# First feed-forward layer of groups 8 to 11: two groups at a time, seven block products of 256 columns in place of eight

## The chip, the core and the metric

The kernel runs on one core of a Trainium2 chip. Its engines work side by side, each through its own queue in order: TensorE (PE, matrix products into PSUM; its weight loads, PEld, overlap them), VectorE (DVE), ScalarE (ACT), GpSimd (POOL) and SyncE (SP), which issues DMAs. The metric is the device time of one execution in microseconds. One more execution was recorded by the hardware profiler.

## What is computed

The reference is block-sparse attention followed by a feed-forward block. B = 4 batches, 8 heads, S = 768 positions, head size 64; model width 512, hidden width 2048.

```python
scores_l = scale * q @ k.T      # kept where |pos_i - pos_j| < 16, else -1e9
scores_s = scale * q @ block_max(k).T + log(32)
a = softmax(concat([scores_l, scores_s]))
x = a @ concat([v, block_mean(v)])
xn = (x - mean) / sqrt(var + 1e-6) * g_ln
out = x + relu(xn @ w_ch1) @ w_ch2
```

## The kernel before

**Tiles.** The 3072 rows are 24 tiles T of 128 rows. Attention works on half tiles t = 0 to 47, four heads each, tile T = t // 2. The feed-forward part works on groups g = 0 to 11 of two tiles.

**Attention.** The first batch (t below 12) works in fp32. From t = 12 on, `load_q` and `load_k` load and split operands into an fp16 high and low part, `qk` makes the scores in PSUM, `softmax` takes the minimum on DVE, a step on POOL and the exponential on ACT into the tile `p`. `transp` casts `p` to fp16 with its residue and transposes both by a DMA on SP. `load_v` splits the values, and `pv` multiplies, adds the parts with a DVE reduction into the tile `x` of the row tile and scales it on POOL. There are XB = 6 buffers for x, so tile T + 6 takes the buffer of tile T, once that is stored.

**Normalisation.** `norm(T)` is `ln`, which writes the normalised tile `xn` (two buffers), and `lnT`, which from tile 4 on casts it to fp16 on ACT, takes the residue on DVE and transposes both with one DMA into `xs`, one tile per group and two buffers.

**Feed-forward.** All weights are held in SBUF as fp16 high and low parts, `wt[1, n]` for the first layer (n = 4 k + c: block k of 512 hidden units, chunk c of 128 of the 512 model columns) and `wt[2, f]` for the second. `g1(s)` with s = 8 g + j makes 256 hidden units for the 256 rows of a group. For each 128 hidden units, 12 matmuls of 256 columns run: four chunks, each high x high, low x high, high x low. ACT then writes `hh` (relu, fp16) and DVE `hl` (the residue). HB = 9 buffers of each let the first layer run ahead. `g2(s)` adds that block to two PSUM accumulators of 512 columns, one a row tile, 12 matmuls in all. After four and after eight blocks DVE adds an accumulator to `x` (it is "drained"), and after eight SP stores x to `out_x`.

**Order.** Every operation is recorded by a planner and nothing is issued when it is called. The planner (`Plan`) knows which operations need which, through tiles and the reuse of their buffers; it simulates the five engines with costs of its own, ranks operations by how late they could start, and repeats this 32 times (`ROUNDS`). What it has then is a fixed order for each engine. So all matmuls have the same line in the profile, L375, the helper that issues them. Extra waiting time that the planner allows for comes from `slack`. The place where a step is called sets which buffer it gets and what it depends on, but not when it runs. In the program's text, group g was called at t = 4 g + 4, when its two tiles are complete.

**Buffers by turn.** `HOMES` lists for some kinds of tile the memory that is taken in turn: three places for `ksg` (loaded k), four for `kh`, two each for `qs`, `p16`, `pT` and `bst`. PSUM has four pools ("s", "o", "h", "a") of two banks. Scores use s, value products o, the first layer h, the second a; the last group's second tile has a further accumulator in o, so that the end can go out in halves.

Of the kernel before, what the change touches and what calls it, by code (L numbers as in the profile page):

```python
# [23 lines left out]
P = 128  # L24
# [21 lines left out]
WARMV = 4  # L46
WARM = 36
PVS = 4


SEQ = [(1 + m // 8 % 2, m % 8 + m // 16 * 8) for m in range(2 * NF)]
# [21 lines left out]
WORDER = (  # L73
# [25 lines left out]
class Plan:  # L99
# [159 lines left out]
    def slack(self, x, y):  # L259

        name, a = self.names[x.stage]
        if x.engine == "tensor":
            if name in ("g1", "g2"):
                return SLACK2 * (a[0] >= 24)
            return SLACK * (name in ("qk", "pv", "batch_s"))
        late = name in ("load_q", "load_k", "load_v", "softmax", "transp", "pv") and a[0] >= LATE
        late |= name[:5] == "batch" and a[0] >= 2
        late |= name in ("ln", "lnT") and a[0] >= LATE // 2
        late |= name in ("g1", "g2") and a[0] >= 24
        if not late:  # L270
            return 0.0
        return SLACKD if y.dma else SLACKE
# [107 lines left out]
def body(ctx: ExitStack, tc, qt, qa, qe, kt, ks, va, vb, vs, g_ln, w1, w2, blocks, out):  # L380
    pl = Plan()
    cp = ctx.enter_context(tc.tile_pool(name="const", bufs=1))
    wp = ctx.enter_context(tc.tile_pool(name="work", bufs=1))
    pools = {n: ctx.enter_context(tc.tile_pool(name="ps" + n, bufs=2, space=bass.MemoryType.PSUM)) for n in "soha"}

    def work(tag, name, shape, dt=F32, bufs=1):
        return pl.tile(wp, shape, dt, tag, name, bufs)

    def psum(tag, name, shape):
        return pl.tile(pools[tag], shape, F32, tag, name, 2)  # L390


    wt = {}

    msk = cp.tile([P, 3, NC], F32, name="msk")
# [3 lines left out]
    tails = [cp.tile([P, 2, 2, NV2], F32, name=f"vst{i}") for i in range(NV)]  # L399
    vst = [x.rearrange("p h v x -> p (h v x)")[:, : 8 * D].rearrange("p (i j d) -> p i j d", i=2, j=4) for x in tails]  # L400
# [18 lines left out]
    kx = [work(f"kx{x}", f"kx{x}", [P, 2, NE])[:] for x in range(2)]  # L419

    emask = work("qke", "emask", [P, 3, NE])[:]

# [34 lines left out]
    @pl.step  # L457
    def go_late():
        late["p"] = prob[0], work("k0_0", "p3", [P, 4, NE])
        for x in late["p"]:  # L460
            nc.gpsimd.memset(x[:, :, NC:], 0.0)
        for i in range(2):
            late["v", i] = work(f"v16_{i}", f"v16_{i}", [P, 2, 4, 2, D], F16)

    def queue(*key):
        return nc.scalar if any(key[: len(x)] == x for x in BESIDE) else nc.sync

    turn = {}

    def home(kind):  # L470
        n = turn[kind] = turn.get(kind, -1) + 1
        return HOMES[kind][n % len(HOMES[kind])]

    stg_n = [0]

    def stg(tag, shape, dt=F32):
        stg_n[0] += 1
        if tag == "bst1":
            tag = ("bst", "qs")[stg_n[0] % 2]
        elif tag in ("bst", "qs"):  # L480
            tag = home(tag)
        return work(tag, f"{tag}{stg_n[0]}", shape, dt, 1 + (tag == "xn"))


# [127 lines left out]
    @pl.step  # L612
    def load_q(t):

        T, hh = divmod(t, 2)
        qs = stg('qs', [P, 4, P])
        for half in range(2):
            nc.sync.dma_start(qs[D * half : D * half + D], qt[T, hh])
        qhl = work(f"qhl{t % 2}", f"qhl{t}", [P, 4, P], F16)
        sc = bt["s", T // NT][:, 1:2]  # L620
        nc.scalar.activation(qhl[:], qs[:], AF.Copy, scale=sc)
        nc.vector.scalar_tensor_tensor(qhl[:D], qs[:D], sc[:D], qhl[:D], ALU.mult, ALU.subtract)
        st[t, "q"] = qhl

    @pl.step
    def load_k(t, pr):
        T, hh = divmod(t, 2)
        b = T // NT
        ksg = work(home("ksg"), f"ksg{t}_{pr}", [P, 2, NC])
# [4 lines left out]
        kh = work(home("kh"), f"kh{t}_{pr}", [P, 2, NC], F16)  # L634
# [33 lines left out]
    @pl.step  # L668
    def softmax(t, pr):
        T = t // 2  # L670
        var = 0 if T % NT == 0 else (2 if T % NT == NT - 1 else 1)
        if pr == 0:
            st[t, "p"] = (prob if t < NEARLY else late["p"])[t % 2]
            st[t, "mn"] = work("mn", f"mn{t}", [P, 4], F32, 2)
            if t >= NEARLY:
                st[t, "sum"] = work("sum", f"sum{t}", [P, 4], F32, 2)
        p, mn, sm, ps = st[t, "p"], st[t, "mn"], st.get((t, "sum")), st[t, "s", pr]
        if t < NEARLY:
            heads = [(2 * pr + v, emask[:, var] if v else msk[:, var]) for v in range(2)]
            for v, (j, mk) in enumerate(heads):  # L680
                w = mk.shape[1]
                nc.vector.tensor_tensor_reduce(
                    p[:, j, :w], ps[:, v, :w], mk, -QSCALE, 3.0e38, ALU.add, ALU.min, mn[:, j : j + 1]
                )
            for j, mk in heads:
                x = p[:, j, : mk.shape[1]]
                nc.scalar.activation(x, x, AF.Exp, bias=mn[:, j : j + 1], scale=-1.0)
            return
        mk = bt["mask", T // NT][:, var]
        for u in range(2):  # L690
            j = 2 * pr + u
            nc.vector.tensor_tensor_reduce(
                p[:, j, :NC], ps[:, u], mk, -1.0, 3.0e38, ALU.add, ALU.min, mn[:, j : j + 1]
            )
        m2, (scale, plus) = mn[:, 2 * pr : 2 * pr + 2], bt["c", T // NT]
        nc.gpsimd.tensor_scalar(m2, m2, plus, 0.0, ALU.mult, ALU.add)
        for u in range(2):
            j = 2 * pr + u
            x = p[:, j, :NC]
            nc.scalar.activation(x, x, AF.Exp, bias=mn[:, j : j + 1], scale=scale, accum_out=sm[:, j : j + 1])  # L700

    @pl.step
    def transp(t):

        p = st[t, "p"]
        p16 = work(home("p16"), f"p16_{t}", [P, 4, 3, P], F16)
# [5 lines left out]
        pT = work(home("pT"), f"pT_{t}", [P, 12, P], F16)  # L712
# [252 lines left out]
    def g2(s):  # L965
# [7 lines left out]
        for i in range(2):  # L973
# [3 lines left out]
            for c, ps in enumerate(acc[i]):  # L977
# [16 lines left out]
                if j == 7:  # L994
                    nc.sync.dma_start(out[T * P : T * P + P, cs], xt[T][:, cs])

    @pl.step
# [41 lines left out]

    def norm(T):  # L1040
        ln(T)
        lnT(T)

    def batch(b):
        for hp in range(4):
# [120 lines left out]
```

## Time and profile before

| | |
|---|---|
| time, median of 3 | 633.95 us (633.9 to 635.35) |
| the profiled execution | 633.53 us, of which the span is 631.7 |
| PE busy | 612.3 us, 97% of the span |
| DVE, ACT, POOL busy | 434.8, 388.2, 212.2 us |
| mean granted PE clock | 0.997 |

The span runs from the first to the last instruction of the recorded execution. A row of the profile names an engine, an operation, and "out<-in" by the program's tiles without their numbers: `h<-xs,wp` is a first-layer matmul, `a<-wp,hh` and `a<-wp,hl` a second-layer one, `o<-v,pT` a value product, `s<-kh,qhl` a score. PE's matmuls are pipelined, so one matmul's own duration is longer than the distance to the next; the distance is what counts for a sum.

### The profile page before, as it was taken

To read this page: it belongs to the slowest core of one execution; us is meant where nothing else is said; L and a number is where in the kernel's file an instruction comes from. 1 tells how busy PE (TensorE), PEld (TensorE's weight loads), DVE (VectorE), ACT (ScalarE), POOL (GpSimd) and SP (SyncE) were. 2 spreads that over 40 slices of the span, in tenths; PEclk is the share of its full clock that TensorE was granted. 3 is DMA by queue.
4 is the path that set the end of the run, shared out by engine and by line. 5 is a ranking of instruction groups with operands and counts; after the bars stand their busy time and mean duration, and the time that the engine had idled before them with its cause. 6 is when DMAs were issued, how large, how long until landed. Compare 5 with 4: busy or idle time off the path is not lost.

```text
span 631.7 us, 13448 instructions
## 1 busy us (share of the span) xinstructions
PE 612.3 (97%) x4678; PEld 435.7 (69%) x4678; DVE 434.8 (69%) x1160; ACT 388.2 (61%) x988; POOL 212.2 (34%) x417
## 2 busy tenths in 40 slices
PE   6899999999999999999999999999999999999997
PEld 5587777675776777666677677667766766666665
DVE  3799999898889999767976766756756744321212
ACT  3698899768998959778774664764663642110100
POOL 5131132022556537534643353533523512100000
PEclk8999999999999999999999999999999999999999
DMA  8990378535999887897755555756646423110000
GB/s 259 337 325 9 105 226 311 184 88 156 249 240 223 192 197 183 170 244 197 191 138 148 125 109 128 150 122 139 151 106 127 108 52 65 20 51 0 20 15 34
DMA packets 126628, 93.15 MB, mean 147 GB/s; under 512 B 84960, under 2 KB 109024, under 8 KB 126560
## 3 DMA queue, kind: packets, MB, share of 16 engines
q1 hardware_dynamic: 124928, 91.50, 56.3%
q10 hardware_dynamic: 1632, 0.79, 0.4%
q8 instruction: 37, 0.61, 0.4%
q14 instruction: 31, 0.25, 0.1%
HBM read 66.27 MB, written 6.29 MB: 115 GB/s over the span
## 4 chain that ended last, share of the span: by engine, by line
PE 56%; DVE 18%; DMA 13%; ACT 5%; issue 4%; POOL 3%; SPq 1%; ACTq 0%; DVEq 0%; POOLq 0%
PE a L375 26%; PE h L375 23%; PE o L375 3%; DMA ksg<-in_kt 3%; PE s L375 2%; DVE wp L375 2%; DVE wf L375 2%; DVE p L375 2%; DMA raw<-in_w 2%; ACT p L375 2%; DVE hl L375 2%; DMA vw<-in_va 2%; DVE x L375 2%; DMA bst<-in_ks 2%; DVE kl L375 2%
## 5 line engine op out<-in xcount | busy, mean ns | idle before, releaser
L375 PE MATMUL h<-xs,wp 128*128 128x256 f16 x2304 | 273.1, 273 | 1.8 <-DMA xs<-x 1.1
L375 PEld LDWEIGHTS <-wp 128*128 128x128 f16 x2304 | 223.8, 98 | 44.1 <-issue 1.8
L375 PE MATMUL a<-wp,hh 128*128 128x512 f16 (+1 forms) x768 | 226.5, 377 | 0.8 <-DVE x L375 0.8
L375 PE MATMUL a<-wp,hl 128*128 128x512 f16 x384 | 144.7, 377 | 0.0
L375 ACT ACTIVATE hh<-h 128x512 f16<-128x512 f32 x96 | 56.8, 592 | 128.6 <-PE h L375 106.6
L375 DVE SCALAR_TENSOR_TENSOR hl<-h,hh 128x512 f16<-128x512 f32 x96 | 65.8, 686 | 91.4 <-ACT hh L375 91.4
L375 PEld LDWEIGHTS <-hh 128*128 128x128 f16 x784 | 75.8, 98 | 64.5 <-issue 1.6
L375 ACT ACTIVATE p<-p,mn,sv 128x184 f32<-128x184 f32 x144 | 76.3, 533 | 20.4 <-POOL mn L375 17.1
L375 POOL TENSOR_TENSOR p<-p,p 128x512 f16<-128x512 f32 x72 | 71.8, 1006 | 25.8 <-ACT p L375 22.1
L375 PEld LDWEIGHTS <-hl 128*128 128x128 f16 x392 | 38.3, 98 | 44.6
L375 DVE CUSTOM_DVE_ANT_0 p<-s,mask 128x184 f32<-128x184 f32 x144 | 43.2, 343 | 21.5 <-PE s L375 21.4
L375 POOL TENSOR_SCALAR mn<-mn,sv 128x2 f32<-128x2 f32 x72 | 33.6, 469 | 66.7 <-DVE mn L375 66.6
L375 ACT ACTIVATE kh<-ksg,sv 128x368 f16<-128x368 f32 x72 | 42.9, 597 | 16.6 <-POOL ksg L375 16.5
L375 DVE SCALAR_TENSOR_TENSOR x<-a,wsc,x 128x512 f32<-128x512 f32 (+1 forms) x48 | 35.3, 738 | 23.6 <-PE a L375 23.6
L375 POOL TENSOR_TENSOR x<-x,rc 128x256 f32<-128x256 f32 x36 | 29.1, 809 | 65.3 <-DVE x L375 65.3
L375 DVE SCALAR_TENSOR_TENSOR kl<-ksg,sv,kh 128x368 f16<-128x368 f32 x72 | 46.3, 668 | 0.1
L375 POOL COPY ksg<-ksum 128x48 f32<-128x48 f32 x72 | 22.0, 307 | 68.1 <-DMA ksg<-in_kt 66.1
L375 ACT CAST p<-p 128x512 f16<-128x512 f32 x72 | 33.6, 509 | 0.4
L375 DVE TENSOR_REDUCE x<-o 128x256 f32<-128x512 f32 x36 | 24.4, 680 | 10.6 <-PE o L375 10.6
L375 DVE SCALAR_TENSOR_TENSOR v<-vst,sv,v 128x512 f16<-128x512 f32 x36 | 27.2, 761 | 0.7 <-ACT v L375 0.7
L375 PEld LDWEIGHTS <-pT 128*128 128x128 f16 x432 | 23.4, 98 | 6.2 <-DMA pT<-p 2.7
L375 PEld LDWEIGHTS <-qhl 128*128 128x128 f16 x288 | 24.0, 98 | 5.2
(127 smaller groups left out, 790.4 us busy)
## 6 DMA issues: line engine op xcount, KB each, us to landing
raw<-in_w SPq DMA_DIRECT2D x32, 512.0 KB, 7.9
ksg<-in_kt SPq DMA_DIRECT2D x72, 184.0 KB, 2.8
out_x<-x SPq DMA_DIRECT2D x23, 256.0 KB, 3.3
qw<-in_qt SPq DMA_DIRECT2D x36, 128.0 KB, 3.0
vst<-in_va SPq DMA_DIRECT2D x36, 128.0 KB, 2.4
qs<-in_qt SPq DMA_DIRECT2D x36, 128.0 KB, 2.8
vst<-in_vb SPq DMA_DIRECT2D x84, 32.0 KB, 2.0
bst<-in_ks SPq DMA_DIRECT2D x12, 192.0 KB, 2.6
```

Of the source, the lines that this page charges most:

```text
L375: getattr(getattr(nc, self.ops[i].engine), op)(*a, **k)
```

## The change

Groups 8 to 11 become two pairs, pn = 4 (tiles 16 to 19) and pn = 5 (tiles 20 to 23). The 512 rows of a pair are two block rows: the even tiles and the odd tiles, 256 rows each. The 512 model columns are two block columns, and 512 hidden units (block k) two blocks of 256. So the first layer of block k is a 2 x 2 block product, which takes eight block products of 12 matmuls each (256 hidden units, 256 rows, 256 model columns in high and low parts). `sp1` makes it from seven, by Winograd's form of Strassen's scheme:

- `combine(k, c)`, called eight times at t = 24, adds high and low parts of two weight chunks on POOL, makes four combinations on DVE and splits them again (ACT, DVE) into `tt[k, c]`, in memory that the first batch and the raw weights used.
- `split1(T)` (even tiles) and `split2(T)` (odd tiles) take the place of `lnT` from tile 16 on. They make a11, a12, a22 and four combinations s1 to s4 of the two tiles, each cast, with residue, and transposed by DMA; pair 4 has 5 transposes per two tiles, pair 5 has 7.
- `sp1(pn, k)` runs the seven products with three PSUM banks. The sums x and z go on growing after they have been read: `note` copies an intermediate sum on ACT, and three DVE additions join the sums. `keep` writes hh and hl.
- `sp2` is the second layer for one block row, with the same number of matmuls as `g2`. `pair_ffn` calls it so that the odd tiles follow every second block.
- Pairs are called at t = 8 pn + 8, that is 40 and 48.

To make room: HB is 8. `kh` has three homes, one of them in the memory of the first batch's kx, beside the scratch tile "room". From t = 42 (`ONE`) on, ksg, qs, p, p16 and pT have a single buffer each (`ALONE`), since pair 5's operands take the second ones. Tiles 22 and 23 have x in `msk` and in `qw4`, not among the six buffers. From t = 28 value products use one PSUM bank, o0. The planner gets slack for the new steps.

```diff
-HB = 9
+HB = 8
+SP = 4
+ONE = 42
-    kh=("kh0", "kh1", "kx0", "kx1"),
+    kh=("kh0", "kh1", None),
+ALONE = dict(ksg=("qke",), qs=("qs",), p16=("p2",), pT=("pta",))
+WD = (("vw0", "vw1"), ("vw2", "vw3"), ("vw4", "vw5"), ("qw2", "qw3"))
+OPS = {
+    4: dict(a11="xs", a12="xs", a22="qw5", s2="xs", s4="xs", s3="room", s1="tail"),
+    5: dict(a11="bst", a12="qw1", a22="k0_0", s2="k0_1", s4="k0_2", s3="k0_3", s1="qw0"),
+}
+XHOME = {22: "msk", 23: "qw4"}
+SLACKP = 500
...
+            if name in ("sp1", "sp2"):
+                return SLACK2 if name == "sp2" or self.names[y.stage][0] != "sp1" else SLACKP
...
-            st[t, "p"] = (prob if t < NEARLY else late["p"])[t % 2]
+            st[t, "p"] = (prob if t < NEARLY else late["p"])[t % 2 if t < ONE else 0]
...
-        ps = psum("o", f"o{t}", [P, 4, 2, D])
+        ps = psum("o", f"o{t}", [P, 4, 2, D], 0 if t >= 8 * SP - 4 else None)
...
-            xt[T] = work("x", f"x{T}", [P, DM], F32, XB)
+            xt[T] = work(XHOME[T], f"x{T}", [P, DM]) if T in XHOME else work("x", f"x{T}", [P, DM], F32, XB)
...
+    def combine(k, c):
+        top, low = (wt[1, 4 * k + 2 * i + c] for i in range(2))
+        yt, yb = work("tail", f"yt{k}_{c}", [P, DM]), late["room"]
+        for y, w in ((yt, top), (yb, low)):
+            nc.gpsimd.tensor_tensor(y[:], w[:, 0], w[:, 1], ALU.add)
+        l, r = slice(0, 256), slice(256, DM)
+        nc.vector.tensor_tensor(yb[:, r], yb[:, r], yt[:, r], ALU.subtract)
+        nc.vector.tensor_tensor(yt[:, r], yt[:, r], yt[:, l], ALU.subtract)
+        nc.vector.tensor_tensor(yt[:, l], yb[:, r], yt[:, l], ALU.add)
+        nc.vector.tensor_tensor(yb[:, l], yb[:, l], yt[:, l], ALU.subtract)
...
+        for y, d in zip((yt, yb), both):
+            nc.scalar.copy(d[:, 0], y[:])
+            nc.vector.tensor_tensor(d[:, 1], y[:], d[:, 0], ALU.subtract)
...
+    def split(x, pn, i, *names):
...
+        nc.scalar.copy(x16[:, :, 0], x)
+        nc.vector.tensor_tensor(x16[:, :, 1], x, x16[:, :, 0], ALU.subtract)
+        for g in (names,) if OPS[pn][names[0]] == OPS[pn][names[-1]] else [(n,) for n in names]:
+            j = names.index(g[0])
+            nc.sync.dma_start_transpose(
+                operand(pn, *g)[:, i], x16[:, j : j + len(g)].rearrange("p o a d -> p (o a d)")
+            )
+    def split1(T):
+        split(st[T, "xn"][:], T // 4, T % 4 // 2, "a11", "a12")
+    def split2(T):
...
+        split(b[:, r], pn, i, "a22")
+        sub(b[:, r], b[:, l], b[:, r], ALU.add)
+        sub(b[:, l], a[:, l], b[:, l])
+        sub(a[:, l], b[:, r], a[:, l])
+        sub(a[:, r], a[:, r], a[:, l])
+        split(a[:], pn, i, "s2", "s4")
+        split(b[:], pn, i, "s3", "s1")
...
+        x = psum("o", f"qx{pn}_{k}", [P, 2, 256], 1)
+        y, z = (psum("h", f"q{n}{pn}_{k}", [P, 2, 256]) for n in "yz")
+        product(x, "a11", plain(0, 0), True)
+        one = note("c22", "one", x)
+        product(y, "a12", plain(1, 0), True, True)
+        nc.vector.tensor_tensor(y[:], y[:], one[:], ALU.add)
+        keep("11", y)
+        product(x, "s2", made(0, 0))
+        two = note("ptb", "two", x)
+        product(z, "s3", made(1, 1), True)
+        seven = note("c22", "seven", z)
+        product(x, "s1", made(0, 1))
+        nc.vector.tensor_tensor(seven[:], x[:], seven[:], ALU.add)
+        keep("22", seven)
+        product(z, "a22", made(1, 0), last=True)
+        nc.vector.tensor_tensor(z[:], z[:], two[:], ALU.add)
+        keep("21", z)
+        product(x, "s4", plain(1, 1), last=True)
+        keep("12", x)
...
+    def pair_ffn(pn):
+        for k in range(4):
+            sp1(pn, k)
+            sp2(pn, k, 0)
+            if k % 2:
+                sp2(pn, k - 1, 1)
+                sp2(pn, k, 1)
...
-        lnT(T)
+        if T < 4 * SP:
+            lnT(T)
+        elif T % 2 == 0:
+            split1(T)
+        else:
+            split2(T)
...
-        while done < NG and t >= 4 * done + 4:
+        while done >= 2 * SP and done < NG and t >= 4 * done + 8:
+            pair_ffn(done // 2)
+            done += 2
+        while done < 2 * SP and t >= 4 * done + 4:
...
+        if t == 24:
+            for n in range(8):
+                combine(n // 2, n % 2)
```

More of the change, by code (lines that the diff above doesn't have):

```diff
@@ L268, in slack @@
         late |= name in ("ln", "lnT") and a[0] >= LATE // 2
-        late |= name in ("g1", "g2") and a[0] >= 24
+        late |= name in ("g1", "g2") and a[0] >= 24 or name in ("sp1", "sp2", "split1", "split2")
         if not late:
@@ L383, in body, with psum @@
     wp = ctx.enter_context(tc.tile_pool(name="work", bufs=1))
-    pools = {n: ctx.enter_context(tc.tile_pool(name="ps" + n, bufs=2, space=bass.MemoryType.PSUM)) for n in "soha"}
+    pools = {n: ctx.enter_context(tc.tile_pool(name="ps" + n, bufs=1, space=bass.MemoryType.PSUM)) for n in "soha"}
+    banks = dict.fromkeys("soha", 0)
     def work(tag, name, shape, dt=F32, bufs=1):
         return pl.tile(wp, shape, dt, tag, name, bufs)
-    def psum(tag, name, shape):
-        return pl.tile(pools[tag], shape, F32, tag, name, 2)
+    def psum(tag, name, shape, at=None):
+        if at is None:
+            at = banks[tag] = 1 - banks[tag]
+        return pl.tile(pools[tag], shape, F32, f"{tag}{at}", name)
     wt = {}
-    msk = cp.tile([P, 3, NC], F32, name="msk")
+    msk = work("msk", "msk", [P, 3, NC])
     gcol = cp.tile([P, 2, 4], F32, name="gcol")
@@ L398, in body @@
     ident = cp.tile([P, P], F32, name="ident")
-    tails = [cp.tile([P, 2, 2, NV2], F32, name=f"vst{i}") for i in range(NV)]
-    vst = [x.rearrange("p h v x -> p (h v x)")[:, : 8 * D].rearrange("p (i j d) -> p i j d", i=2, j=4) for x in tails]
+    tails = [cp.tile([P, 2, 2, NV2], F32, name=f"vst{i}") for i in range(NV - 1)]
+    tails.append(work("tail", "tail", [P, 2, 2, NV2]))
+    vst = [x.rearrange("p h v x -> p (h v x)")[:, : 8 * D].rearrange("p (i j d) -> p i j d", i=2, j=4) for x in tails[:2]]
     ones = cp.tile([P, P], F32, name="ones")
@@ L418, in body @@
     vend = work("bst", "vend", [BLK, DM])[:]
-    kx = [work(f"kx{x}", f"kx{x}", [P, 2, NE])[:] for x in range(2)]
+    kxs = work("kx", "kx", [P, 2, 2, NE])
+    kx = [kxs[:, x] for x in range(2)]
     emask = work("qke", "emask", [P, 3, NE])[:]
@@ L463, in go_late @@
             late["v", i] = work(f"v16_{i}", f"v16_{i}", [P, 2, 4, 2, D], F16)
+        room = work("kx", "room", [P, 4 * NE], F32)
+        late["room"] = room[:, :DM]
+        late["kh"] = room[:, DM : DM + NC].bitcast(F16).rearrange("p (u c) -> p u c", u=2)
     def queue(*key):
@@ L468, in body, with home, stg @@
     turn = {}
-    def home(kind):
+    def home(kind, t=0):
         n = turn[kind] = turn.get(kind, -1) + 1
-        return HOMES[kind][n % len(HOMES[kind])]
+        n, homes = (0, ALONE) if t >= ONE and kind in ALONE else (n % len(HOMES[kind]), HOMES)
+        return homes[kind][n]
     stg_n = [0]
-    def stg(tag, shape, dt=F32):
+    def stg(tag, shape, dt=F32, t=0):
         stg_n[0] += 1
@@ L628, in load_k @@
         b = T // NT
-        ksg = work(home("ksg"), f"ksg{t}_{pr}", [P, 2, NC])
+        ksg = work(home("ksg", t), f"ksg{t}_{pr}", [P, 2, NC])
         nc.sync.dma_start(ksg[:], kt[T, hh, pr])
@@ L633, in load_k @@
         )
-        kh = work(home("kh"), f"kh{t}_{pr}", [P, 2, NC], F16)
+        at = home("kh")
+        kh = work(at, f"kh{t}_{pr}", [P, 2, NC], F16) if at else late["kh"]
         kl = work("kl", f"kl{t}_{pr}", [P, 2, NC], F16, 2)
@@ L995, in g2 @@
                     nc.sync.dma_start(out[T * P : T * P + P, cs], xt[T][:, cs])
+    ops, tt, quad = {}, {}, {}
+    @pl.step
+    def combine(k, c):
[8 more added lines that the diff above has]
+        nc.vector.tensor_tensor(yb[:, l], yb[:, l], yt[:, l], ALU.subtract)
+        n = 2 * k + c
+        if n < 4:
+            both = work(f"ring{n}", f"wd{n}", [P, 2, 2, DM], F16)
+            both = [both[:, i] for i in range(2)]
+        else:
+            both = [work(x, f"wd{n}_{x}", [P, 2, DM], F16) for x in WD[n - 4]]
+        for y, d in zip((yt, yb), both):
+            nc.scalar.copy(d[:, 0], y[:])
+            nc.vector.tensor_tensor(d[:, 1], y[:], d[:, 0], ALU.subtract)
+        tt[k, c] = both
@@ new lines, in operand @@
+    def operand(pn, *names):
+        tag = OPS[pn][names[0]]
+        if names[0] not in ops.setdefault(pn, {}):
+            shape, bufs = [P, 2, 4 * len(names), P], 1 + (tag == "xs")
+            x = late["room"].bitcast(F16).rearrange("p (i c k) -> p i c k", i=2, c=4) if tag == "room" else work(tag, f"op{pn}_{names[0]}", shape, F16, bufs)
+            for j, n in enumerate(names):
+                ops[pn][n] = x[:, :, 4 * j : 4 * j + 4]
+            ops[pn][names] = x
+        return ops[pn][names]
@@ new lines, in sp1, with product, plain, made @@
+    @pl.step
+    def sp1(pn, k):
+        def product(ps, x, w, first=False, last=False):
+            for u in range(2):
+                with pl.unit():
+                    for n in range(6):
+                        c, (a, b) = n // 3, ((0, 0), (0, 1), (1, 0))[n % 3]
+                        nc.tensor.matmul(
+                            ps[:, u, :], w(c, a, u), ops[pn][x][:, :, 2 * b + c],
+                            start=(first and u == 0 and n == 0), stop=(last and u == 1 and n == 5), skip_group_check=True,
+                        )
+        def plain(i, j):
+            return lambda c, a, u: wt[1, 4 * k + 2 * i + c][:, a, 256 * j + P * u : 256 * j + P * u + P]
+        def made(i, j):
+            return lambda c, a, u: tt[k, c][i][:, a, 256 * j + P * u : 256 * j + P * u + P]
+        def keep(name, x):
+            hh = work("hh", f"hh{name}{pn}_{k}", [P, 2, 256], F16, HB)
+            hl = work("hl", f"hl{name}{pn}_{k}", [P, 2, 256], F16, HB)
+            nc.scalar.activation(hh[:], x[:], AF.Relu)
+            nc.vector.scalar_tensor_tensor(hl[:], x[:], 0.0, hh[:], ALU.max, ALU.subtract)
+            quad[pn, k, name] = hh, hl
+        def note(tag, name, x):
+            t = work(tag, f"{name}{pn}_{k}", [P, 2, 256])
+            nc.scalar.copy(t[:], x[:])
+            return t
+        x = psum("o", f"qx{pn}_{k}", [P, 2, 256], 1)
[17 more added lines that the diff above has]
+        keep("12", x)
@@ new lines, in sp2 @@
+    @pl.step
+    def sp2(pn, k, v):
+        last = pn == TT // 4 - 1 and k >= 2 and v == 1
+        if k % 2 == 0:
+            tag = "s" if pn == TT // 4 - 1 and v else "a"
+            st["acc", pn, v] = [[psum(tag, f"a{pn}_{k}_{v}_{i}", [P, DM])] for i in range(2)]
+            if last:
+                st["acc", pn, v][1].append(psum("o", "last", [P, DM], 0))
+        for i in range(2):
+            T, acc = 4 * pn + 2 * i + v, st["acc", pn, v][i]
+            parts = len(acc)
+            for c, ps in enumerate(acc):
+                cs = slice(DM // parts * c, DM // parts * (c + 1))
+                for j in range(2):
+                    hh, hl = quad[pn, k, f"{v + 1}{j + 1}"]
+                    with pl.unit():
+                        for u in range(2):
+                            f = 4 * k + 2 * j + u
+                            for n, (h, a) in enumerate(((hh, 0), (hh, 1), (hl, 0))):
+                                nc.tensor.matmul(
+                                    ps[:, : DM // parts],
+                                    h[:, u, i * P : i * P + P],
+                                    wt[2, f][:, a, cs],
+                                    start=(k % 2 == 0 and j == 0 and u == 0 and n == 0),
+                                    stop=(k % 2 == 1 and j == 1 and u == 1 and n == 2),
+                                )
+                if k % 2 == 1:
+                    nc.vector.scalar_tensor_tensor(
+                        xt[T][:, cs], ps[:, : DM // parts], kout[:, k // 2 : k // 2 + 1], xt[T][:, cs], ALU.mult, ALU.add
+                    )
+                if k == 3:
+                    nc.sync.dma_start(out[T * P : T * P + P, cs], xt[T][:, cs])
```

17 lines of the change are left out of this document (13 added, 4 removed).

## The prediction

> **What bounds the kernel now.** I read the page first: the engines' totals and the clock.
>
> ```profile
> span 631.7 us, 13448 instructions
> ...
> PE 612.3 (97%) x4678; PEld 435.7 (69%) x4678; DVE 434.8 (69%) x1160; ACT 388.2 (61%) x988; POOL 212.2 (34%) x417
> ...
> PEclk8999999999999999999999999999999999999999
> ```
>
> TensorE is busy for 97% of the span at its full clock after the first slice. A matmul's busy time overlaps its neighbour's, so this alone doesn't say that it is dense. The waits of PE from 286 us to the end do:
>
> ```profile
> PE h L375 <- DMA xs<-x: 1.1, 1, 1.1
> ```
>
> That one wait of 1.1 us is all in 345 us. The chain of waits gives the pace without overlap:
>
> ```profile
> 577.56 2.62 PE h L375 x24
> 580.18 2.59 PE a L375 x12
> ```
>
> A first-layer matmul (256 columns) takes 2.62/24 = 0.109 us of PE, a second-layer one (512 columns) 2.59/12 = 0.216 us. Then the stages, as busy time by stretch (columns: stretch, its length, then PE, PEld, DVE, ACT, POOL with counts, clock, DMA share, GB/s):
>
> ```profile
> 150.00:265.00 115.00, 112.70 (x940) 82.62 (x938) 101.99 (x277) 98.97 (x263) 62.10 (x111) 1.00 0.89 208
> ...
> 300.00:430.00 130.00, 130.00 (x1015) 91.39 (x1014) 92.00 (x248) 82.49 (x202) 55.69 (x97) 1.00 0.60 139
> ...
> 480.00:550.00 70.00, 70.00 (x536) 47.48 (x535) 39.18 (x98) 28.10 (x67) 20.63 (x33) 1.00 0.38 73
> ```
>
> From 150 to 265 us VectorE (89%) and ScalarE (86%) are nearly full too; from 300 on PE alone is, with VectorE at 71% and then 56%. So a PE instruction removed after 300 us shortens the end one for one, as long as the data that PE needs come in time. That condition is where this change can fail.
>
> **What sets the pace of attention.** In the late part attention isn't held by its own engines. It waits for tiles of x: the output of tile T and the attention of tile T+6 share a buffer (XB = 6). Around tiles 12 and 18, then 14 and 20:
>
> ```profile
> 429.85 1.65 SPq L375 DMA_DIRECT2D out_x<-x  x2
> ...
> 476.32 1.65 SPq L375 DMA_DIRECT2D out_x<-x  x2
> ```
> ```profile
> L375 PE MATMUL o<-v,pT x144: 192/219/220, 432.8 to 547.4; 128*128 128x128 f16 x96, 128*128 128x64 f16 x48
> ```
> ```profile
> 479.25 0.73 PE L375 MATMUL o<-v,pT 128*128 128x128 f16 x12
> ```
>
> The value product of tile 18 starts at 432.8, 3.0 us after the store that frees its x; that of tile 20 at 479.25, 2.9 us after its. From half tile 40 at 479.25 to half tile 47 at 546.80 (its row is further down) there are 7 pitches in 67.6 us, 9.65 us each. In the crowded stage it was shorter:
>
> ```profile
> L375 PE MATMUL o<-v,pT x132: 192/219/230, 170.0 to 258.9; 128*128 128x128 f16 x88, 128*128 128x64 f16 x44
> ```
>
> 132 are 11 half tiles, 10 pitches from 170.0 to about 258.3 (the last one takes 0.6 us): 8.8 us each, with the double buffers.
>
> **What is removed.**
>
> ```profile
> L375 PE MATMUL h<-xs,wp 128*128 128x256 f16 x2304 | 273.1, 273 | 1.8 <-DMA xs<-x 1.1 <-DVE wsc L375 0.7
> ```
>
> 2304 over 12 groups is 192 a group, 384 for two. The seven products have 7 x 12 = 84 matmuls of the same shape per block of 512 hidden units, four blocks a pair: 336. Two pairs save 2 x 48 = 96 matmuls x 0.109 = **10.5 us** of PE. The second layer keeps its 192 per pair. A pair is then 336 x 0.109 + 192 x 0.216 = 36.7 + 41.4 = 78.1 us of PE.
>
> **What is added, engine by engine.** Durations from the groups by shape:
>
> ```profile
> L375 DVE SCALAR_TENSOR_TENSOR hl<-h,hh 128x512 f16<-128x512 f32 x96 | 65.8, 686 | 91.4 <-ACT hh L375 91.4
> L375 ACT ACTIVATE hh<-h 128x512 f16<-128x512 f32 x96 | 56.8, 592 | 128.6 <-PE h L375 106.6 <-PE a L375 21.6
> ...
> L375 POOL TENSOR_TENSOR p<-p,p 128x512 f16<-128x512 f32 x36 | 45.4, 1262 | 25.7 <-ACT p L375 22.1 <-DMA ksg<-in_kt 1.7 <-POOL x L375 1.4
> ...
> L375 POOL TENSOR_TENSOR p<-p,p 128x256 f16<-128x256 f32 x36 | 27.0, 750 | 0.1
> ...
> L375 ACT CAST p<-p 128x256 f16<-128x256 f32 x36 | 14.6, 405 | 0.0
> L375 DVE TENSOR_TENSOR x<-xn,x 128x512 f16<-128x512 f32 x20 | 14.1, 707 | 2.1 <-ACT x L375 2.1
> L375 ACT CAST x<-xn 128x512 f16<-128x512 f32 x20 | 12.3, 615 | 13.7 <-DVE xn L375 13.7
> ...
> L375 DVE TENSOR_TENSOR x<-o,rc 128x256 f32<-128x256 f32 x4 | 1.7, 416 | 0.0
> ```
>
> combine, eight times: 2 POOL adds of 512 (1.26 each), 4 DVE differences of 256 (0.42), 2 ACT casts (0.62) and 2 DVE residues (0.71). In all POOL 20.2, DVE 8 x 3.08 = 24.7, ACT 9.8 us. split1 and split2, per two tiles: ACT 3 casts of 512 and one of 256 = 2.25 (was 1.23); DVE 3 residues of 512, 5 operations of 256 = 4.20 (was 1.41). Over four such pairs ACT +4.1, DVE +11.2. sp1: the sixteen relus and residues of a pair of groups stay sixteen; new are 3 copies out of PSUM (0.59 by the relu's row) and 3 adds (0.69) in each of 8 blocks: ACT +14.2, DVE +16.5. DVE goes from 434.8 to 487 us, ACT to 416, POOL to 232. No engine but PE becomes the bound. combine is in the program at half tile 24 and is needed only at about 450 us. In the stretch from 300 to 430 VectorE has 38 us idle and POOL 74, which hides it. Without that cover it costs at most its chain of some 7 us a call, and attention pays it, not PE directly. On SyncE the transposes of normalised tiles 16 to 23 grow from 8 to 10 + 14 = 24. One is a 1.24 us issue that lands after 3.1 us:
>
> ```profile
> L375 SPq DMA_TRANSPOSE xs<-x x20: 1233/1242/1607, 138.7 to 554.2; - x20
> ...
> DMA to landing us min/median/max: 3.1/3.1/4.9
> ```
>
> 16 more are at most 20 us of a queue, between 400 and 540 us. Behind them wait the loads of the next half tiles. HB = 8, the third home of kh, one PSUM bank for the late value products and msk as a shared tile: I cost each at nothing. What hides it is second-layer work, of which up to eight blocks stand ready for PE; a missing hh buffer would cost one first-layer step, 2.6 us.
>
> **The new turns in PSUM.** In sp1 the sums x and z are read while they are still being built, so each next product into x waits for a copy or an add. The profile has no such wait. The nearest rows are an ordinary evacuation near the end, where nothing else runs:
>
> ```profile
> 619.04 1.47 PE L375 MATMUL h<-xs,wp 128*128 128x256 f16 x12
> ...
> 620.55 0.60 ACT L375 ACTIVATE hh<-h 128x512 f16<-128x512 f32 x1 [3.30 <-PE h L375]
> ...
> 621.19 0.69 DVE L375 SCALAR_TENSOR_TENSOR hl<-h,hh 128x512 f16<-128x512 f32 x1 [2.48 <-ACT hh L375]
> ```
>
> The matmuls end at 620.51, the read at 621.15: 0.64 us. The product in between is 12 x 0.109 = 1.31 us, so 0.67 us is to spare, and one operation of 0.6 us ahead of the copy on its engine just fits. Below, the cost is nothing. Above, every one of 6 turns in 8 blocks could lose 0.5 us: 24 us. A gain is excluded, since a wait can't make PE quicker. I take 0.1 us for each of the 24 turns of the first pair, beside which attention uses the same queues, and nothing in the second: **2.4 us**. That is near the lower end, as the row has more to spare than it needs.
>
> **The deadline.** A pair starts only when all its four tiles are normalised and combined. Before, group 10 could start without tiles 22 and 23. The last matmul and the end:
>
> ```profile
> 628.08 0.27 PE L375 MATMUL last<-wp,hl 128*128 128x256 f16 x1
> ```
>
> leave 3.6 us to 631.7. For the full saving the span is 621.2, so pair 5 must start by 621.2 - 3.6 - 78.1 = 539.5 us. Before, tile 23's transpose was issued at 554.2 and landed near 557.3, which is 18 us too late. split2 lengthens the chain by about 4 us (four operations of 0.42, one more cast and residue of 0.62 and 0.71, one further issue of 1.24: 4.2); the two products a11 and a12 need only split1 and give back 2.6. What can move it ahead: tiles 22 and 23 get their own x (msk and qw4), so the gate is tile 20 alone, that is, the end of group 7. While pair 4 runs, PE also has attention's own matmuls. By the busy time of the scores' matmuls,
>
> ```profile
> 430.00:550.00 120.00, 6.38 (x64) 0.00 (x0) 14.69 (x44) 1.00 0.44 97
> ```
>
> (the figure after the length is PE; 64 matmuls are 8 half tiles, 0.8 us each), and 0.73 for a value product, that is some 9 us for six half tiles. So PE ends group 7 at about 539.5 - 78.1 - 9 = 452 us. Then value product 40 is at 452 + 3 = 455 instead of 479, and at the old pitch product 47 is at 455 + 7 x 9.65 = 522.5. From product 47 to landing it took
>
> ```profile
> 546.80 0.69 PEld L375 LDWEIGHTS <-pT 128*128 128x128 f16 x12
> ...
> 550.97 0.55 DVE L375 TENSOR_SCALAR xn<-x,mv,rs 128x512 f32<-128x512 f32 x1 [0.96 <-POOL rs L375]
> ```
>
> 557.3 - 546.8 = 10.5 us; with 4 more, pair 5 can start at 537 and, less 2.6, at 534.5. That is 5 us inside the deadline. Pair 4 must start by 452 as well. Tile 19's transpose was issued at
>
> ```profile
> L375 SPq DMA_TRANSPOSE xs<-x x2: 1233/1252/1270, 443.8 to 459.3; - x2
> ```
>
> 459.3, landing at 462.4. With 4 more and 2.6 less it has to come some 12 us earlier, by ending group 6 earlier. The ready second-layer work allows this, as PE no longer has group 8 to begin with. I count no wait at either pair.
>
> **Sum.** 631.7 - 10.5 + 2.4 = 623.6 us of span. Outside the span the profiled execution has 633.53 - 631.7 = 1.8, and it is 0.4 below the median of 633.95: 623.6 + 1.8 + 0.4 = **625.8 us**.
>
> **Rivals.** *First: single-buffered attention makes pair 5 wait (slower).* From half tile 42 on p, its fp16 copy, its transpose and the loads have one buffer each. A half tile's chain through p is then serial: two pairs of DVE and ACT steps, POOL's two differences (1.26 and 0.75 us), a transpose. The pitch may grow from 9.65 to 12 or 13 us. At 13 from product 41 on: 455 + 9.6 + 6 x 13 = 542.6, start at 542.6 + 14.5 - 2.6 = 554.5, span 554.5 + 78.1 + 3.6 = 636.2, time 638.4. If tile 23 doesn't move at all it is 557.3 + 4 - 2.6 + 81.7 = 640.4, time 642.6. It decides from a pitch of (539.5 - 11.9 - 455)/7 = 10.4 us upwards; slower than before by more than 0.3% begins at some 12.6. For it: the chain rests on four margins at once. Against it: the pitch of 9.65 was itself stretched by waits for x, and 8.8 was reached on fuller engines. The Trainium skill's rule "Double-buffer for performance" (Trainium Kernel Development and Optimization, Best Practices) speaks for this rival; the trace of before has no single-buffered stretch to show it. PE would also stand idle then: the skill's page TensorE: Matmul & The Clock Gate (HAM oscillation) says that a gap over some 3.4 us halves the clock for the next window. The clock row shows no such drop after the start, with no wait above 1.1 us late; by that rule this rival would be about 1.7 us dearer still.
>
> *Second: the turns stall (about no change or slower).* If other work stands ahead of the copies on ScalarE and VectorE at all 48 turns, at 0.3 us each, it is 14.4 instead of 2.4: 637.8 us. Against it: PE has second-layer matmuls of 1.3 us to put between, and beside pair 5 no attention is left.
>
> *Third: pair 4 waits (part of the gain).* If tile 19 lands only 4 us earlier than before, the pair starts at 462.4 - 2.6 = 459.8 and PE idles 7.8 us: 633.6. For it: nothing in the profile of before shows group 6 ending early. Against it: the order is planned anew, and no first layer of group 8 is there to go ahead of group 7's second.
>
> **How the numbers follow.** Forecast 0.60 (622 to 630 by itself: all turns free, up to 4 us of waiting); first rival 0.22; second 0.10; third 0.08. The range takes in the unknown turns and most of the first rival up to a pitch of about 12.5: 622 to 638. This kernel's measurement can tell about 0.3% (1.9 us) from no change. Faster than 632.05: all of the first, a fifth of the first rival, a third of the others: 0.69. Within 0.3%: 0.10. Slower: 0.21.
>
> **What would show it.** First-layer matmuls 2304 - 96 = 2208 at 0.109 us of pitch. The last value product near 523 us and the first product that needs tile 23 before 540; if PE's waits show one of several us for a transposed operand near 540, the first rival holds. Waits of PE for ACT copies or DVE adds inside sp1 should sum to under 5 us; if they reach 15, the second. VectorE near 487 us busy. A store of group 7 later than 460 us would put my account of the gate wrong. A time above 632 makes the forecast wrong.

## The result and the profile after

| | before | after |
|---|---|---|
| time, median of 6 runs each | 635.83 us | 627.7 us (627.31 to 632.16) |
| ratio after/before, 95% interval | | 0.9879 (0.984 to 0.9919) |
| the recorded execution | 633.53 us, span 631.7 | 632.16 us, span 630.2 |

The changed kernel is faster by 1.2%, between 5 and 10 us. Its recorded execution is an unlucky one: the other five runs took 627.3 to 628.0 us. A second recording of the same kernel, made for the experiments, took 625.84 us. Both are shown, since their difference turned out to be part of the answer. First the page of the recorded execution after the change:

```profile
span 630.2 us, 13470 instructions
...
PE 605.9 (96%) x4572; PEld 428.6 (68%) x4572; DVE 492.0 (78%) x1256; ACT 408.8 (65%) x1036; POOL 238.0 (38%) x433
...
PEclk9899999979999999997999999999999999999999
...
L387 PE MATMUL h<-xs,wp 128*128 128x256 f16 x1536 | 183.5, 275 | 1.8 <-DVE hl L387 1.5
```

PE has 106 matmuls fewer (4678 to 4572): the 96, and ten fillers without a result (`spare`, 67 before and 57 after). VectorE rose to 492 us and POOL to 238. The clock row has two slices at 0.7 where the profile of before had none; what stands behind them is shown with the experiments. The page of the second recording:

```profile
span 623.9 us, 13470 instructions
...
PE 603.2 (97%) x4572; PEld 429.2 (69%) x4572; DVE 491.2 (79%) x1256; ACT 408.6 (65%) x1036; POOL 240.3 (39%) x433
```

and what PE waited for in it from 300 us to the end:

```profile
PE qz L387 <- DMA op_s<-x_s: 0.2, 1, 0.2
```

0.2 us in 324: neither the turns in PSUM nor the start of pair 5 makes PE wait. The same question to the first recording gives 0.5 us, for the same operand. Pair 4, and the last value product (rows of the second recording, in order of time):

```profile
449.24 0.53 SPq L387 DMA_DIRECT2D out_x<-x  x1
...
462.46 0.37 SPq L387 DMA_DIRECT2D out_x<-x  x1
```
```profile
451.17 0.73 PE L387 MATMUL o<-v,pT 128*128 128x128 f16 x12
451.73 1.47 PE L387 MATMUL qx<-op_a,wp 128*128 128x256 f16 x12
```
```profile
521.07 0.73 PE L387 MATMUL o<-v,pT 128*128 128x128 f16 x12
...
526.19 1.47 PE L387 MATMUL qx<-op_a,wp 128*128 128x256 f16 x12
...
537.23 1.47 PE L387 MATMUL qx<-op_s,wd 128*128 128x256 f16 x12
538.93 1.47 PE L387 MATMUL qz<-op_s,wd 128*128 128x256 f16 x12 [0.22 <-DMA op_s<-x_s]
```

The first product of pair 4 starts at 451.73, value product 47 at 521.07, the first product that needs tile 23 at 537.23. Between 526 and 537 PE works off second-layer blocks of pair 4, beside pair 5's two products of a11 and a12, which need even tiles alone. The only trace of the deadline is the wait of 0.22 us at 538.9: tile 23 comes just in time.

### The profile page after: what moved, and what is told of

Its sections match the earlier page's. It is cut to its first block, busy times and chain, and to the rows that moved or that the text cites. A ratio compares the mean times of both kernels' runs of the same rounds, so it can differ in the third digit from the quotient of the medians.

```text
span 630.2 us, 13470 instructions
## 1 busy us (share of the span) xinstructions
PE 605.9 (96%) x4572; PEld 428.6 (68%) x4572; DVE 492.0 (78%) x1256; ACT 408.8 (65%) x1036; POOL 238.0 (38%) x433
## 4 chain that ended last, share of the span: by engine, by line
PE 71%; DVE 13%; DMA 9%; ACT 3%; issue 2%; SPq 1%; POOL 1%; ACTq 0%; DVEq 0%; POOLq 0%
PE a L387 33%; PE h L387 19%; PE qx L387 6%; PE s L387 4%; PE o L387 3%; PE qz L387 3%; DVE wf L387 3%; DVE wp L387 2%; DMA raw<-in_w 2%; DMA vw<-in_va 2%; DMA bst<-in_vs 2%; DVE hl L387 1%; DMA ksg<-in_kt 1%; DVE raw L387 1%; PE qy L387 1%
## 5 line engine op out<-in xcount | busy, mean ns | idle before, releaser
L387 PEld LDWEIGHTS <-wp 128*128 128x128 f16 x1824 | 178.6, 99 | 35.9 <-issue 4.2
L387 PE MATMUL h<-xs,wp 128*128 128x256 f16 x1536 | 183.5, 275 | 1.8 <-DVE hl L387 1.5
L387 PE MATMUL a<-wp,hl 128*128 128x512 f16 (+1 forms) x384 | 145.7, 380 | 0.0
L387 POOL COPY ksg<-ksum 128x48 f32<-128x48 f32 x72 | 28.1, 393 | 64.5 <-DMA ksg<-in_kt 60.3
L387 DVE SCALAR_TENSOR_TENSOR hl<-h,hh 128x512 f16<-128x512 f32 x64 | 43.4, 679 | 11.2 <-ACT hh L387 11.1
L387 ACT ACTIVATE hh<-h 128x512 f16<-128x512 f32 x64 | 37.5, 586 | 14.7 <-PE h L387 14.5
L387 ACT ACTIVATE kh<-ksg,sv 128x368 f16<-128x368 f32 x48 | 28.3, 594 | 15.1 <-POOL ksg L387 13.5
L387 DVE SCALAR_TENSOR_TENSOR kl<-ksg,sv,kh 128x368 f16<-128x368 f32 x48 | 32.1, 673 | 0.9 <-ACT kh L387 0.9
L387 DVE SCALAR_TENSOR_TENSOR v<-vst,sv,v 128x512 f16<-128x512 f32 x36 | 29.6, 823 | 3.7 <-ACT v L387 3.7
L387 ACT ACTIVATE v<-vst,sv 128x512 f16<-128x512 f32 x36 | 25.6, 715 | 3.7 <-PE o L387 3.2
```

The costliest lines, as they stand in the source:

```text
L387: getattr(getattr(nc, self.ops[i].engine), op)(*a, **k)
```

## Where the rest of the 10.5 us went: experiments

All ratios are to the kernel before on the same chip, with 95% intervals; 0.1% is 0.63 us.

**The changed kernel again.**

> The changed kernel once more, unaltered. Its recorded execution was 632.2 us, while five others were 627.3 to 628.0, and its clock stood at half for two stretches of 6.8 us, after pauses of PE at 124 and at 283 us. Theory A (the 96 matmuls count one for one, and what is missing of the 10.5 us was lost before 300 us, in pauses of PE and in the halved clock behind them): ratio about 0.988, PE's waits after 300 us under 1 us in sum, and the time that is missing stands in pauses and half clock before 300. Rival B (the turns in PSUM or the start of pair 5 took it): waits of 2 us or more after 440 us.

Measured: 0.9914 (0.988 to 0.9948), single runs from 625.84 to 631.16 us: a smaller gain than the 0.9879 measured first, though inside its interval. PE's waits after 300 us are 0.2 us, as theory A had it, so rival B falls. In the recording with 632.16 us, most of the missing time stands here (busy time by stretch of 7 us: PE, PEld, DVE, ACT, POOL, clock, DMA, GB/s):

```profile
280.00:287.00 7.00, 4.90 (x39) 2.77 (x38) 4.10 (x11) 4.55 (x11) 4.26 (x8) 1.00 0.99 249
287.00:294.00 7.00, 5.92 (x24) 3.13 (x22) 5.93 (x10) 7.00 (x19) 2.38 (x4) 0.51 1.03 243
294.00:301.00 7.00, 7.00 (x56) 5.09 (x55) 6.57 (x19) 6.29 (x19) 4.19 (x7) 1.00 0.97 226
```

and this is PE ahead of the middle row:

```profile
283.53 0.38 PE L387 MATMUL a<-wp,hl 128*128 128x512 f16 x1
284.89 0.25 PE L387 MATMUL s<-kh,qhl 128*128 128x184 f16 x1 [0.98 <-DVE mn L387]
286.23 0.24 PE L387 MATMUL s<-kl,qhl 128*128 128x184 f16 x1 [1.08 <-DVE kl L387]
...
288.22 1.01 PE L387 MATMUL h<-xs,wp 128*128 128x256 f16 x4 [1.08 <-DVE hl L387]
```

From 283.5 to 288.2 us PE does nothing but one set of eight score matmuls, with three waits of about 1 us. All three are for VectorE: for `mn` (the minimum of scores), for `kl` (the low part of k) and for `hl`. VectorE is late here, yet in the first row it is busy for only 4.10 of the 7 us, while the share of the DMA engines is 0.99. Ahead of this ScalarE had waited for a load,

```profile
280.40 0.63 ACT L387 ACTIVATE bst<-bst 128x512 f32<-128x512 f32 x1 [1.42 <-DMA bst<-in_qa]
```

and VectorE then waited 3.23 us for ScalarE. From the third wait on the clock stands at half, for the whole of the next stretch (0.51). In the second recording of the same program ScalarE doesn't wait for that load, and only the last of PE's three waits is there, of 0.75 us:

```profile
284.21 1.47 PE L387 MATMUL h<-xs,wp 128*128 128x256 f16 x12 [0.75 <-DVE hl L387]
```

The clock stays full there, and the span is 6.3 us shorter. PE's order is the same in both recordings, so its instructions can be laid side by side: the first recording is 1.1 us behind at 277 us and 6.2 us behind at 306 us. So this is one place with two outcomes, and it makes up 5 of the 6.3 us. The first slice at 0.7 in the clock row stands behind a wait up to 127 us, 3.1 us against 2.6 in the second recording. The Trainium skill (TensorE: Matmul & The Clock Gate, HAM oscillation) gives the rule that PE gaps over some 3.4 us halve the clock for a time. The halving agrees, the condition doesn't, and the measurement decides: no wait of PE at this place is over 1.1 us, and the three together are 3.1 us.

**The room alone.** The buffers as in the changed kernel, but no pair:

```diff
-SP = 4
+SP = 6
-        ps = psum("o", f"o{t}", [P, 4, 2, D], 0 if t >= 8 * SP - 4 else None)
+        ps = psum("o", f"o{t}", [P, 4, 2, D], 0 if t >= 28 else None)
-        if t == 24:
+        if t == 24 and SP < 6:
```

> Only the room is made: eight hh buffers, three homes of kh, single buffers from half tile 42, x of tiles 22 and 23 apart, one bank for late value products. No group is paired, no weights are combined; the first layer has its 2304 matmuls. Theory A in its first form (the room slows attention before 300 us, chiefly the third home of kh): 2 to 4 us slower than before, ratio 1.003 to 1.006, with the transposes of tile 11 later than 282 us. Rival (the room is free, as the prediction has it): ratio 0.998 to 1.002.

Measured: 1.0042 (1.0017 to 1.0066), 2.7 us slower than before. The room is not free. The rival, which was the prediction's own term, falls. From 300 us on PE waits for nothing in its recording. Before 300 us it has a wait that the kernel before doesn't have at all, the first layer's for `hl`:

```profile
PE h L387 <- DVE hl L387: 5.9, 6, 2.0
```

Tile 11 is later, as expected:

```profile
L387 SPq DMA_TRANSPOSE xs<-x x2: 1447/1954/2461, 284.8 to 292.2; - x2
```

These are tiles 10 and 11, at 284.8 and 292.2 (before: tile 11 at 282.4).

**Eight products.** The product of a12 is made twice, the second over the first:

```diff
         product(y, "a12", plain(1, 0), True, True)
+        product(y, "a12", plain(1, 0), True, True)
```

> The changed kernel with an eighth product: the product of a12 is made twice, the second over the first, so that only 96 matmuls of PE come back. If PE bounds from 300 us on, it is 10.5 us slower than the changed kernel: ratio to before about 1.004. If pair 5 waits for its data in the changed kernel, part of the 10.5 is hidden: ratio 0.995 or less.

Measured: 1.0049 (1.0025 to 1.0072). That is 1.35% or 8.6 us over the changed kernel (0.9914), and with both intervals (0.34 and 0.24 points) between 6 and 11 us: 10.5 is inside. The one-for-one account stands within that. It also equals the room alone (1.0042) within the intervals, which leave some 2 us open: beyond that, pairs, combinations, operands and turns together cost nothing, and the seventh against the eighth product is the whole gain.

**No combinations.** Products that should use combined weights take plain ones, which changes the output; combine isn't called:

```diff
-            return lambda c, a, u: tt[k, c][i][:, a, 256 * j + P * u : 256 * j + P * u + P]
+            return plain(i, j)
...
-            for n in range(8):
-                combine(n // 2, n % 2)
+            pass
```

> The changed kernel without the weight combinations: the products that should use them take plain weights, so the output differs; 20 us of POOL, 25 of DVE and 10 of ACT are left out. Theory C (that work, done early because its engines take whatever is ready, delays attention before 300 us): 2 to 4 us faster than the changed kernel, ratio to before 0.982 to 0.985. If it is hidden, as the prediction has it: the same as the changed kernel within 1 us, ratio 0.987 to 0.990.

Measured: 0.9919 (0.9894 to 0.9944), above both ranges, but the same as the changed kernel's 0.9914 on that chip. Within the intervals, some 2.7 us, the combinations are hidden, and nothing speaks for theory C. In the changed kernel they ran spread over a long time (second recording):

```profile
L387 POOL TENSOR_TENSOR yt<-wp x8: 1147/1156/1723, 139.2 to 386.5; 128x512 f32<-128x512 f16 x8
```

**Two pieces of the room, put into the kernel before.**

```diff
-    kh=("kh0", "kh1", "kx0", "kx1"),
+    kh=("kh0", "kh1", "kx0"),
```

> The kernel before with three homes of kh (kh0, kh1, kx0) in place of four, and nothing else. The room alone cost 0.42% (2.7 us), and tile 11's transpose came at 292 instead of 282 us. Theory A1 (the third home does it: the split of the next k has to wait for scores one and a half half tiles back): ratio 1.003 to 1.006, tile 11's transpose at 287 us or later. Rival A2 (it is the ninth hh buffer, or the new plan as a whole): ratio 0.998 to 1.002, tile 11's transpose near 282.

```diff
-HB = 9
+HB = 8
```

> The kernel before with eight hh and hl buffers in place of nine, and nothing else. Theory A2 (the first layer runs one step less ahead, so PE stands idle while attention is late, 2.6 us a time): ratio 1.003 to 1.006 and pauses of PE between 200 and 300 us larger than the 3.3 us before. Theory A1: ratio 0.998 to 1.002.

Measured: 1.0101 (1.0066 to 1.0136) for the third home of kh, 1.007 (1.0041 to 1.0098) for eight hh buffers. By its middle value each alone costs more than the whole room (1.0042), though the intervals touch or overlap. And A1's own mark is missing: with three homes tile 11's transpose is at 282.6, where it was before.

```profile
L375 SPq DMA_TRANSPOSE xs<-x x1: 1257/1257/1257, 282.6 to 282.6; - x1
```

A2's mark hardly shows: with eight hh buffers the pauses of PE between 200 and 300 us sum to 4.1 us, against the 3.4 of the kernel before. So neither A1 nor A2 stands as it was put. Both edits cost, but not by a sum of parts. What they share with the room alone is PE's wait for `hl` before 300 us: nothing in the kernel before, 3.7 us with three homes, 3.2 with eight buffers, 5.9 with the whole room. Each edit makes the planner write a new order for every engine. That the cost depends on that order too is my reading; no run holds the order fixed.

**A fourth home of kh in the changed kernel**, in 0.7 KB a partition that was unused; run twice, the second time beside the changed kernel once more.

```diff
-    kh=("kh0", "kh1", None),
+    kh=("kh0", "kh1", None, "kh3"),
```

> The changed kernel with a fourth home of kh in memory of its own (0.7 KB a partition, which was free). Theory A1: the attention before 300 us is back at its old pace, and it is 2 to 3 us faster than the changed kernel, ratio to before 0.986 to 0.989. A2: as the changed kernel, 0.990 to 0.993.

> The changed kernel, unaltered, to stand beside the next one on the same chip: ratio to before 0.988 to 0.992.

> The changed kernel with the fourth home of kh, once more. If the third home is a cause of what is missing: 2 to 4 us faster than the changed kernel on the same chip, ratio to before 0.983 to 0.988. If the earlier difference was chance: 0.989 to 0.992.

Measured: 0.9858 (0.9825 to 0.9891) and 0.9848 (0.9822 to 0.9874), beside it the changed kernel with 0.9871 (0.9838 to 0.9905). The pair on one chip has medians of 624.16 against 625.28 us: 1 us, less than the 2 to 4 expected, since the changed kernel itself came out faster than the 0.988 to 0.992 that I had put down. The two intervals overlap, so the gain over the changed kernel is likely but not settled. Nor is attention back at its old pace, as A1 had it: tile 11's transpose is at 290.7 and 290.5 us with four homes, 289.6 in the changed kernel's second recording and 282.4 before. So this mark doesn't tell what the room costs. The wait for `hl` before 300 us goes better with the times: 0.2 us in both recordings with four homes, 1.3 to 1.6 in the three of the changed kernel. It isn't the whole of it, since the run without combinations has 5.9 us of it at the changed kernel's time. What the recordings also show is the place at 283 us. With four homes (first row) PE is full there, in the changed kernel's third recording (second and third row) it isn't:

```profile
278.00:285.00 7.00, 7.00 (x58) 4.65 (x56) 5.22 (x15) 6.02 (x17) 3.72 (x8) 1.00 0.99 242
```
```profile
278.00:285.00 7.00, 5.13 (x41) 3.07 (x39) 4.04 (x11) 4.39 (x10) 4.13 (x8) 1.00 0.86 226
285.00:292.00 7.00, 6.06 (x25) 3.34 (x24) 5.87 (x11) 6.86 (x20) 1.90 (x3) 0.52 1.06 242
```

The spans are 623.1 and 629.4 us. On this chip the runs spread accordingly: 622.8 to 625.2 us with four homes, 623.7 to 631.4 without (with four homes on another chip, 622.3 to 627.2). By its medians this version is the fastest of the three kernels.

An account by work says the same. First- and second-layer matmuls issued before 300 us, at 0.109 and 0.216 us each:

| | first layer | second | us of PE | span |
|---|---|---|---|---|
| before | 1022 | 396 | 197 | 631.7 |
| room alone | 968 | 408 | 194 | 636.6 |
| changed, second recording | 981 | 408 | 195 | 623.9 |
| changed, first | 960 | 393 | 190 | 630.2 |
| changed, third | 960 | 401 | 191 | 629.4 |
| changed, four homes (again) | 971 | 414 | 195 | 623.1 |

From 300 us on PE is full in all of them. The two bad recordings of the changed kernel have 4 to 6 us less done by then than the second one, and end 5.5 to 6.3 us later.

**The gate of x.** Tiles 22 and 23 back among the six shared buffers:

```diff
-XHOME = {22: "msk", 23: "qw4"}
+XHOME = {}
```

> The changed kernel with x of tiles 22 and 23 among the six shared buffers again, so that they wait for the stores of tiles 16 and 17, which pair 4 gives at about 534 and 557 us. If x is the gate of attention, as the deadline's working has it: the last value product moves from 521 to about 565 us, pair 5's products for tile 23 start near 578 instead of 526 to 540, PE waits some 40 us there, and the time is about 670 us. If attention is held by something else (its engines, or the planner's order): within 5 us of the changed kernel.

Measured once: 642.87 us (before on that chip: 633.82). The waits of PE after 300 us begin with

```profile
PE qx L387 <- DMA op_s<-x_s: 5.1, 1, 5.1
```

and the last value product comes at 552.2 instead of 521.6:

```profile
L387 PE MATMUL o<-v,pT x168: 192/219/230, 402.7 to 552.2; 128*128 128x128 f16 x112, 128*128 128x64 f16 x56
```

The gate is there, and attention ends 30 us later for it. But the longest wait is 5.1 us, and all waits after 300 us sum to some 11 us and not 40, so the time lies between the two answers that I had expected: I had left the order of pair 4 as it was, while the planner moved the stores of pair 4 ahead (two at 528 and 540, all by 549, where the changed kernel has 534 to 557) and kept second-layer work for the gap.

**Single buffers from half tile 30.**

```diff
-ONE = 42
+ONE = 30
```

> The changed kernel with single buffers of attention from half tile 30 on instead of 42. In the changed kernel the last four value products came 12 us apart, the ones before 8.4. First rival's mechanism (single buffers make attention slower than PE's own pace of about 10 us a half tile): at 12 us from half tile 30, which is at about 361 us, product 47 comes at 361 + 17 x 12 = 565, pair 5 waits some 40 us, and the time is 660 us or more; at 11 us it is 548 and about 645. If single buffers cost nothing by themselves (the pitch at the end is that of PE's queue and of the planner): product 47 by 525 us and a time within 3 us of the changed kernel.

Measured: 1.0136 (1.0105 to 1.0167), median 642.18 us. Value products of half tiles 30 to 47, in this kernel and in the changed one (second recording):

```profile
L387 PE MATMUL o<-v,pT x216: 192/219/220, 337.5 to 547.5; 128*128 128x128 f16 x72, 128*128 128x64 f16 x36
```
```profile
L387 PE MATMUL o<-v,pT x216: 192/219/220, 347.5 to 521.6; 128*128 128x128 f16 x72, 128*128 128x64 f16 x36
```

Without the last block's 0.5 us these are 17 pitches of 12.3 and of 10.2 us: the slower pitch is as the first rival put it. That the single buffers force it isn't shown, since half tiles 43 to 45 of this run, single-buffered too, come 8.4 and 9.0 us apart. And no wait of PE for a transposed operand of pair 5 came of it. The 14 us were lost before 300 us (880 and 396 matmuls issued there, 181 us of PE), where nothing is single-buffered yet; the planner had drawn attention forward, and the first layer stood still once:

```profile
202.37 0.73 PE L387 MATMUL o<-v,pT 128*128 128x128 f16 x12
208.65 5.30 PE L387 MATMUL h<-xs,wp 128*128 128x256 f16 x24 [5.55 <-DVE hl L387]
```

A pause of 5.6 us, and then 24 first-layer matmuls have 5.30 us in their row, against 2.78 in a row of 24 at the full clock (second recording, at 286.81): the clock is at half again. So this run doesn't price single buffers by themselves; both answers that I had expected are missed.

**Three pairs** (groups 6 to 11), pair 3 with pair 4's operand memory:

```diff
-SP = 4
+SP = 3
 OPS = {
+    3: dict(a11="xs", a12="xs", a22="qw5", s2="xs", s4="xs", s3="room", s1="tail"),
```

> Strassen's products for three pairs (groups 6 to 11): 48 first-layer matmuls less than the changed kernel, 5.2 us of PE. Pair 3 takes the same operand memory as pair 4, so pair 4's operands can be made only when pair 3's last product is done, and they need some 12 to 16 us (two tiles of about 4 us of DVE each, and their transposes), with 15 us of second-layer work of pair 3 left for PE. If that work covers it: 5 us faster than the changed kernel, ratio to before 0.983. If not, PE waits between the pairs, and at the next deadline too: 5 to 15 us slower than the changed kernel, ratio 0.999 to 1.015. I hold the second for likelier, as first-layer buffers (eight) can't hold more.

Measured: 1.0104 (1.0076 to 1.0133), 640.58 us, in the second range expected. After 300 us PE waits 13 us in all, of which the first two rows are

```profile
PE a L388 <- DVE x L388: 3.2, 1, 3.2
PE qx L388 <- DMA op_a<-x_a: 2.6, 1, 2.6
```

the second for the first operand of a pair, and the clock halves once more, at 453 us. The second-layer work left between pairs doesn't cover making the next operands in the same memory.

## Why the prediction was right, and where it was off

**The time.** 625.8 us was forecast, with 622 to 638; measured 627.7. As a difference, 8.1 us were forecast against 633.95; the ratio says 7.7 (5 to 10). The same kernel had 0.9914 and 0.9871 in the two later measurements, that is 5.5 and 8.2 us, so the forecast lies at the upper end of what was measured. The chances for a time below 632.05 add up to 0.70, not 0.69.

**The 96 matmuls, 10.5 us.** Right: the eighth product brought 8.6 us back (6 to 11), and after 300 us PE waits 0.5, 0.2 and 1.4 us in the three recordings of the changed kernel and 0.2 us in that of eight products.

**The turns, 2.4 us.** Too high: in the recordings of the changed kernel they show at most 0.3 us of wait for a copy, in the third:

```profile
PE qx L387 <- ACT two L387: 0.3, 1, 0.3
```

Second-layer matmuls stand between the products. The second rival is out.

**The room, nothing.** This term failed. "HB = 8, the third home of kh, one PSUM bank ... I cost each at nothing. What hides it is second-layer work": the room alone cost 2.7 us (1.1 to 4.2). The cover that I named exists after 300 us. The room is also in force before 300, where my own stretch table had VectorE at 89%, ScalarE at 86% and a DMA share of 0.89, and where PE waits when these are late: 5.9 us for `hl` with the room alone, nothing in the kernel before. I had read that table and drawn no price from it. The two misses, 2.4 too much and 2.7 too little, nearly cancel, so the good forecast owes something to luck. What part of the room does it isn't settled: the mark that I gave for the third home failed, the parts don't add up, and a fourth home takes the pauses at 283 us away in one order.

**combine, nothing.** Right (0.9919 against 0.9914), though it ran from 139 to 405 us and not only in the idle time after 300 that I named. VectorE 487 forecast, 491 and 492 measured; ACT 416 and 409; POOL 232 and 240.

**The deadline** (second recording; in the first all of this is 6 us later). Pair 4 forecast from 452, measured 451.7; value product 47 forecast at 522.5, measured 521.1; the pitch 9.65 forecast, (521.07 - 451.17)/7 = 10.0 measured. The first product for tile 23 was possible at 534.5 by my sum and came at 537.2. One step was wrong: I had group 7 end as a whole at 452 and named a store later than 460 as its refutation. Tile 14 was stored at 449.2, tile 15 at 462.5. Pair 4's first products and group 7's last second-layer blocks share the time; value product 40 needs tile 14 alone, so the sum held all the same. The limit was also softer than 539.5, since PE spent most of 526 to 537 on second-layer blocks of pair 4, which I had put ahead of pair 5.

**First rival.** A pitch of 12 does appear where single buffers act (12.3 from half tile 30 on), and at the end of the changed kernel as well, where the last four pitches average 12.3 us (from 472.0 to 521.1). There it came late enough to cost 0.2 us of waiting. Single pitches of 8.4 us stand among them in both kernels, so whether the buffers or the planner's order set the mean stays open. The Trainium skill advises to double-buffer (Trainium Kernel Development and Optimization, Best Practices); the mean pitch goes that way, but no run here shows what single buffers cost in time. Third rival: no wait at pair 4.

## What to carry to other kernels

When memory is taken from an early stage to pay for a gain in a late one, price it in the early stage, where PE still waits for other engines and for loads, and not where the gain lies. With an order written by a planner, an edit of one buffer count changes every queue, and here two single pieces each came out dearer than the whole; measure the making of room as a kernel of its own. A saving on a full engine can pay one for one (here 8.6 us of 10.5, 6 to 11) as long as other work, here a second layer, is held back for the moments at which data arrive.

## What the runs showed of the hardware

Short waits of PE close together were followed by a halved clock. In the first recording of the changed kernel two waits of 0.98 and 1.08 us and eight score matmuls fill the time from 283.9 to 287.1 us; the clock falls as the third wait begins, and the stretch of 7 us from there stands at 0.51. In the third recording the waits are 0.79, 1.08 and 0.90 us, and the stretch at 0.52. A single wait of 1.1 us (the profile of before) or of 1.7 us (the first recording with four homes) passed without effect. A single wait of 2.6 us, at 128 us in the second recording, was followed by 0.76 over 126 to 133 us. So the same program met the place at 283 us in two ways: in two of three recordings the clock halved there, and the spans were 629.4 and 630.2 against 623.9 us.
